# Hash attention and SwiGLU on one core: the second half of batch 1 takes its heads in turn with the first, and one more pair of heads is transposed by VectorE

## The chip, the core and the metric

The kernel runs on one core of one Trainium2 chip. The metric is the device time of one execution in microseconds (us). Before the change three runs gave 336.68, 337.49 and 340.18 us; their median is 337.49 us.

The core's engines run their own instruction streams in program order and meet at semaphores: TensorE (PE, matmuls and transposes), VectorE (DVE), ScalarE (ACT), GpSimd (POOL) and SyncE (SP, which in this kernel only issues DMAs). POOL issues the weights' DMAs.

## What is computed

The first half is attention with a hash mask, the second a gated feed-forward layer (FFN) over its rows. Cut to what matters:

```python
# q, k, v: (4 batches, 8 heads, 768 tokens, 64); proj: (64, 6)
q_bucket = sum over the 6 columns of (q @ proj > 0) * 2**column      # k_bucket likewise
scores = (q @ k.T) / 8
scores = where(q_bucket[:, None] == k_bucket[None, :], scores, -1e9)
attn = softmax(scores)                       # with 1e-9 added to the sum
attn_out = attn @ v
x = attn_out, heads side by side             # (3072, 512)
xn = x / sqrt(mean(x*x) + 1e-6) * rms_g
g = xn @ w_gate                              # 512 -> 1536
out = (g * sigmoid(g) * (xn @ w_val)) @ w_out
```

## The kernel before, in words

**Tiles.** The 768 queries of a batch are cut into two halves of 384, so there are eight windows `w` = 0 to 7, and window `w` belongs to batch `w // 2`. The eight heads of a batch are taken as four pairs `hp`; "(b,hp)" below is a pair of heads of batch b, "w2" is window 2. For each head of a window the 768 keys are taken in three parts.

**Attention.** One tile `QK` per pair holds, for each of its heads, 76 rows: 64 rows of q or k in fp16, transposed, and 12 rows of hash bits, so that one matmul gives score and mask together. `scores` (L338-347) is two matmuls of 384 columns, `probs` (L349) the exponential on ACT, `av` (L357) nine of the 18 matmuls with v, `attn_out` (L373) the division by the sum: VectorE writes `otmp` and `rcp`, POOL `x` and its square `sq` (for the last pair of w0 VectorE does all of it), and `sumsq` (L404) adds the squares up on VectorE.

**Preparing a pair** has two ways, told apart by the list `BY_PE` (L40).
- By PE: k and q come as rows, one DMA of 384 KB each (`load_rows`). `keep_pair` (L539) is called four times a pair, each time three fp32 transposes on PE and a copy out of PSUM by VectorE. `casts` (L543) writes fp16 into `QK`, by POOL, with a quarter of it on ACT. `hash_pair` (L585) makes the hash of both heads.
- By VectorE: k and q come in blocks of 32 columns, four DMAs of 96 KB each for k and for q (`load_blocks`, L115). `turn_dve` (L187) is called eight times a pair, four for k and four for q, each time one VectorE transpose of 128x192. `cast_pool` (L198) writes fp16 on POOL, two instructions for k and two for q. The hash of one pair is `hash_lone` (L273), that of two pairs `hash_pairs` (L288).
Either hash is matmuls `d_ps` on PE (L209), a comparison `bits` on VectorE (L216) and eight DMAs on SP that put the bits into `QK`, for one pair by `hash_pair` and `hash_lone` of 12x384, for two by `hash_pairs` of 12x768. The v of a pair is one DMA; `v_prep` (L307) casts it and `v_sum` (L311) adds it up, both on POOL; `v_mean` (L319) is a matmul of those sums and a VectorE copy `cvb`.

**FFN of a window.** `norm` (L410) makes the root mean square on VectorE and POOL, `scale_x` (L420, three times) `xn` on VectorE, `turn_x` (L425, three times) transposes it on PE and VectorE scales it into `xnT`. Then 12 steps `gate` (L436, four matmuls, tanh on ACT) and `value` (L450, four matmuls; VectorE makes `a` and then `ht`), and `project` (L464, nine calls of four matmuls; ACT copies the result out and SP stores it).

**The order** is written out by hand. `SLOTS` lists 192 slots, one per window, head and part of the keys; `plan[s]` holds what else is emitted in slot s, sorted by a rank. In slot s come `scores(s + 1)`, then the steps with rank under 3, then `probs(s + 1)`, then the others (L699-709). Every engine and each DMA queue runs its share in that order. The FFN of window w starts at slot 24w + 48: the first 16 slots from there hold gates and values, slots +16 to +24 the projection. So slots 48 to 63 carry gates and values of w0, 64 to 72 its projection, 72 to 87 those of w1, and so on.

`TURNS` (L33) gives the order of pairs in batch 0: w0 and w1 take turns. From w2 on a window's heads follow one another: w2 has slots 48 to 71, w3 72 to 95. Six pairs are in `BY_PE`: all of batch 0, (1,0) and (1,1).

**Buffers.** Loaded rows go through ten buffers (`lpool`, L61), each freed by its transposes or by `v_sum`. Banks of PSUM for everything but scores and `o_ps` are three (`gps`), so that a gate's matmuls wait until VectorE is done with a bank used three users before. `xpool` and `xnT` have two buffers, `xn` one. DMAs of SP share eight completion semaphores in turn, so that a DMA waits for the eighth one before it.

Of the kernel before, what the change touches and what calls it, by code (L numbers as in the profile page):

```python
# [15 lines left out]
H = 8  # L16
# [14 lines left out]


TURNS = [(0, 0), (1, 0), (0, 1), (1, 1), (0, 2), (0, 3), (1, 2), (1, 3)]  # L33
SLOTS = [(w, 2 * hp + hh, p) for w, hp in TURNS for hh in range(2) for p in range(3)]
SLOTS += [(w, h, p) for w in range(2, 8) for h in range(H) for p in range(3)]
NS = len(SLOTS)
LAST = {(w, h): g for g, (w, h, p) in enumerate(SLOTS) if p == 2}


BY_PE = [(0, hp) for hp in range(4)] + [(1, 0), (1, 1)]  # L40


@with_exitstack
def kernel(
# [12 lines left out]
    nc = tc.nc  # L57
# [40 lines left out]
    def raw_tile(b, hp, which):  # L98
        shape = [128, 24, 32] if which != "v" and (b, hp) not in BY_PE else [128, 2, 6, D]
        raw[b, hp, which] = lpool.tile(shape, FP32, name=which + "L", tag="L")  # L100
        return raw[b, hp, which]
# [39 lines left out]
    def k_cols(b, h, jt):  # L141
        o = (jt // 3) * S + (jt % 3) * 128 if (b, h // 2) in BY_PE else S + jt * 128
        return QK[b, h // 2][0:KROWS, h % 2, o : o + 128]

    def q_cols(w, h):
        b, half = divmod(w, 2)
        t = QK[b, h // 2][0:KROWS, h % 2]
        if (b, h // 2) in BY_PE:
            return t[:, half * S + HALF : (half + 1) * S]
# [4 lines left out]
    def v_chunk(b, h, jt):  # L154
        return 2 * (jt % 3) + jt // 3 if (b, h // 2) in BY_PE else jt

# [181 lines left out]
    def scores(g):  # L338
        w, h, p = SLOTS[g]
        ps = scps.tile([128, 2, 512], FP32, name="s_ps")  # L340
        idle(ps[:, 0, HALF:512], {0: 8, 3: 6}.get(g, 0))
        for j in range(2):
            nc.tensor.matmul(  # L343
                ps[:, j, 0:HALF], k_cols(w // 2, h, 2 * p + j), q_cols(w, h),
                start=True, stop=True,
            )
        sps[g] = ps

    def probs(g):  # L349
        w, h, p = SLOTS[g]  # L350
        if p == 0:
            psb[w, h] = ppool.tile([128, 3, 2, HALF], FP16, name="psb")
        nc.scalar.activation(  # L353
            psb[w, h][:, p], sps.pop(g)[:, :, 0:HALF], AF.Exp, scale=ESCALE,
        )
# [217 lines left out]
    def at(s, f, *a, rank=3):  # L573
        plan[s].append((rank, len(plan[s]), lambda: f(*a)))
# [39 lines left out]
        at(33 + 6 * i, load_wo, 6 * i, 6 * i + 6)  # L614

    for hp, loads, turns, sv in ((0, (9, 11, 15), (24, 26, 28, 30), 42),
                                 (1, (13, 17, 28), (33, 35, 37, 39), 45)):
        for which, s in zip("kqv", loads):  # L620
            at(s, load_rows, nc.sync, 1, hp, which)
        for i, s in enumerate(turns):
            at(s, keep_pair, 1, hp, i)
            at(s + 1, casts, 1, hp, i)
        at(turns[3] + 2, hash_pair, 1, hp)
        at(sv, v_prep, 1, hp)
        at(sv + 2, v_sum, 1, hp)

    def in_row(loads, s, hash_slot=None):
        return loads, range(s, s + 8), (s + 4, s + 8, s + 9), hash_slot

    work = {
        (1, 2): ((21, 23, 30), (36, 37, 40, 40, 48, 49, 50, 51), (42, 52, 46), 53),
        (1, 3): in_row((42, 44, 47), 52, 61),
        (2, 0): in_row((51, 56, 59), 61), (2, 1): in_row((64, 67, 70), 71, 80),
        (2, 2): in_row((73, 76, 79), 81), (2, 3): in_row((82, 85, 88), 91, 100),
        (3, 0): in_row((94, 98, 102), 106), (3, 1): in_row((104, 108, 112), 116, 125),
        (3, 2): in_row((116, 120, 124), 126), (3, 3): in_row((126, 130, 134), 136, 145),  # L640
    }
    for (b, hp), (loads, turns, cast_slots, sh) in work.items():
        for which, s in zip("kqv", loads):
            at(s, load_rows if which == "v" else load_blocks, nc.sync, b, hp, which)
        for i, s in enumerate(turns):
            at(s, turn_dve, b, hp, "kq"[i // 4], i % 4, rank=5)
        for which, s in zip("kq", cast_slots):
            at(s, cast_pool, b, hp, which)
        if sh:
            if b == 1:  # L650
                at(sh, hash_lone, b, hp)
            else:
                at(sh, hash_pairs, b, (hp - 1, hp))
        at(cast_slots[2], v_prep, b, hp)
        at(cast_slots[2], v_sum, b, hp)
        if hp % 2:
            at(66 if b == 1 else 48 * b + (17 if hp == 3 else -4), v_mean, b, hp - 1, 4)
    at(54, v_mean, 1, 0, 4)

    gts, sqs = {}, {}  # L660

# [13 lines left out]
    for w in range(8):  # L675
        for h in range(H):
            end = LAST[w, h] + 3
            at(end - 1, av, w, h, 0, 9)
            at(end, av, w, h, 9, 18)
            if h % 2:  # L680
                at(end, o_step, w, h // 2, rank=4.5)
                if (w, h) != (0, 7):
                    at(end + 6, s_step, w, h // 2, rank=5)
        at(end + (1 if w == 0 else 9), norm, w, rank=5)
        for c in range(3):
            at(end + (3 if w == 0 else 14 + c), scale_x, w, c, rank=5)
            at(end + (7 + c if w == 0 else 17 + 2 * c), turn_x, w, c, rank=1)
        s0 = 24 * w + 48
        seen = set()
        for ft in range(NF):  # L690
            for f, s in ((g_step, s0 + 16 * ft // NF), (v_step, s0 + (32 * ft + 16) // (2 * NF))):
                at(s, f, w, ft, rank=4 if s in seen else 2)
                seen.add(s)
        for i in range(9 if w < 7 else 6):
            c, j = divmod(i, 3)
            at(s0 + 16 + i, project, w, c, 4 * j, 4 * j + 4, rank=1 if i == 8 else 3)
# [61 lines left out]
```

## Time and profile before

| | before |
|---|---|
| runs | 336.68, 337.49, 340.18 us; median 337.49 |
| the profiled execution | 339.3 us, its span 337.5 us |
| granted TensorE clock | 0.999 |
| PE busy | 326.8 us (97%) |
| VectorE, ScalarE, POOL busy | 236.4 (70%), 210.0 (62%), 155.3 (46%) us |
| PE busy in 40 to 50, 50 to 60, 60 to 70 us | 8.98, 9.32, 7.84 of 10 us |
| PE busy in 70 to 80 and 80 to 90 us | 9.93, 10.00 of 10 us |
| chain that ended last | PE 85%, VectorE 6%, SP's queue 3%, DMA 2%, ACT 2% |

The span is the time from the first to the last instruction in the profile; the device time of that execution is 1.8 us longer. Times in rows of the timeline count from the span's start. A row gives the start, the busy time, the engine, the line, what is written and read, the count, and in brackets the idle time before it and what ended that. "PE" rows last until the result is out, so two of them overlap; the distance from start to start is what a matmul holds the engine for. "SPq" is SP's DMA queue.

### The profile page before, as it was taken

The numbers are of one execution on the slowest core, as the hardware profiler recorded it, in microseconds if no ns is written. First come the engines' busy times: TensorE is split into PE (matmuls) and PEld (weight loads), VectorE is DVE, ScalarE is ACT, GpSimd is POOL, SyncE is SP. The second block draws the span as 40 slices with busy tenths as digits, with TensorE's granted clock in tenths as the row PEclk, the third lists the DMA queues.
The fourth block names the chain that finished last, engine by engine and source line by source line (L and its number), as shares of the span: only waits on it lengthen the run. The fifth ranks groups of instructions, "written<-read, shape, count | busy, mean of one in ns | idle before, by whom it ended". The sixth has DMA issues, their size and how long they took to land.

```text
span 337.5 us, 7796 instructions
## 1 busy us (share of the span) xinstructions
PE 326.8 (97%) x2993; PEld 201.0 (60%) x2993; DVE 236.4 (70%) x526; ACT 210.0 (62%) x328; POOL 155.3 (46%) x230
## 2 busy tenths in 40 slices
PE   8999989889999999999999999999999999999995
PEld 7566656455566565566555666566556665655653
DVE  4769798688758896668768897557546663883860
ACT  3789987656666575757666676567667675332321
POOL 4878789836465576245736475613111311110000
PEclk9999999999999999999999999999999999999999
DMA  7999999464376064508243261100010001001002
GB/s 238 330 223 260 169 169 187 75 124 100 79 186 118 15 111 119 104 20 168 69 105 84 44 116 64 35 16 0 33 62 2 3 0 64 33 0 64 32 0 93
DMA packets 80244, 31.36 MB, mean 93 GB/s; under 512 B 65240, under 2 KB 77264, under 8 KB 80208
## 3 DMA queue, kind: packets, MB, share of 16 engines
q1 hardware_dynamic: 76272, 26.09, 31.7%
q0 software_dynamic: 3712, 4.72, 8.8%
q8 instruction: 23, 0.38, 0.5%
q14 instruction: 13, 0.11, 0.1%
q10 hardware_dynamic: 224, 0.07, 0.1%
HBM read 28.32 MB, written 6.29 MB: 103 GB/s over the span
## 4 chain that ended last, share of the span: by engine, by line
PE 85%; DVE 6%; SPq 3%; DMA 2%; ACT 2%; issue 1%; DVEq 0%; ACTq 0%
PE y_ps L469 18%; PE v_ps L455 17%; PE s_ps L343 15%; PE g_ps L445 12%; PE o_ps L365 9%; PE s_ps L445 5%; PE d_ps L209 4%; SPq L267 2%; PE t_ps L169 1%; PE x_ps L430 1%; PE z_ps L336 1%; DMA kL<-in_k_dram 1%; DVE otmp L380 1%; DVE xn L423 1%; ACT psb L353 1%
## 5 line engine op out<-in xcount | busy, mean ns | idle before, releaser
L353 ACT ACTIVATE psb<-s_ps 128x768 f16<-128x768 f32 x192 | 150.8, 808 | 28.1 <-PE s_ps L343 26.9
L343 PE MATMUL s_ps<-QK 76*128 76x384 f16 x384 | 93.5, 325 | 1.3 <-ACT psb L353 0.5
L455 PE MATMUL v_ps<-xnT,wv 128*128 128x384 f16 x384 | 78.1, 326 | 0.1
L469 PE MATMUL y_ps<-wo,ht 128*128 128x512 f16 x276 | 69.2, 379 | 0.3 <-ACT ysb L476 0.3
L389 POOL TENSOR_TENSOR x<-otmp,rcp 128x384 f32<-128x384 f32 x31 | 25.7, 830 | 93.0 <-DVE rcp L385 92.7
L365 PEld LDWEIGHTS <-psb 128*128 128x128 f16 x1152 | 51.6, 97 | 25.5 <-issue 7.5
L447 ACT ACTIVATE t<-g_ps 128x384 f32<-128x384 f32 x72 | 35.3, 490 | 43.6 <-PE g_ps L445 43.4
L458 DVE SCALAR_TENSOR_TENSOR ht<-a,v_ps 128x384 f16<-128x384 f32 x96 | 53.2, 554 | 10.7 <-PE v_ps L455 1.5
L457 DVE SCALAR_TENSOR_TENSOR a<-t,g_ps 128x384 f32<-128x384 f32 x72 | 39.5, 548 | 28.5 <-ACT t L447 28.3
L445 PE MATMUL g_ps<-xnT,wg 128*128 128x384 f16 x288 | 58.6, 325 | 0.7 <-DVE a L457 0.5
L365 PE MATMUL o_ps<-vl,psb 128*128 128x65 f16 x1152 | 56.8, 194 | 0.6 <-DVE otmp L380 0.5
L455 PEld LDWEIGHTS <-wv 128*128 128x128 f16 x384 | 36.4, 97 | 23.9 <-issue 0.5
L445 PEld LDWEIGHTS <-wg 128*128 128x128 f16 x384 | 36.0, 97 | 24.4 <-issue 1.1
L343 PEld LDWEIGHTS <-QK 76*128 76x128 f16 x384 | 31.6, 98 | 16.1 <-issue 3.7
L469 PEld LDWEIGHTS <-ht 128*128 128x128 f16 x276 | 25.9, 97 | 24.0 <-issue 0.6
L476 ACT COPY ysb<-y_ps 128x512 f32<-128x512 f32 x23 | 13.5, 585 | 25.5 <-PE y_ps L469 22.8
L431 DVE TENSOR_TENSOR xnT<-x_ps,gcol 128x512 f16<-128x512 f16 x24 | 16.3, 685 | 15.1 <-PE x_ps L430 15.1
L401 POOL TENSOR_TENSOR sq<-x 128x384 f32<-128x384 f32 x31 | 25.6, 826 | 2.4
L380 DVE TENSOR_TENSOR otmp<-o_ps,cvb 128x390 f32<-128x390 f32 x32 | 17.8, 558 | 8.8 <-PE o_ps L365 8.7
L447 ACT ACTIVATE t<-s_ps 128x384 f32<-128x384 f32 x24 | 11.8, 491 | 18.4 <-PE s_ps L445 17.6
L201 POOL CAST QK<-kT 64x768 f16<-64x768 f32 x20 | 16.8, 838 | 12.4 <-DVE kT L193 6.5
L193 DVE STREAM_TRANSPOSE kT<-kL 128x192 f32<-128x192 f32 x40 | 19.8, 517 | 2.7 <-DMA kL<-in_k_dram 2.7
(80 smaller groups left out, 325.7 us busy)
## 6 DMA issues: line engine op xcount, KB each, us to landing
vL<-in_v_dram SPq DMA_DIRECT2D x16, 384.0 KB
out_dram<-ysb SPq DMA_DIRECT2D x23, 256.0 KB
kL<-in_k_dram SPq DMA_DIRECT2D x40, 96.0 KB
qL<-in_q_dram SPq DMA_DIRECT2D x40, 96.0 KB
kL<-in_k_dram SPq DMA_DIRECT2D x5, 384.0 KB
qL<-in_q_dram SPq DMA_DIRECT2D x5, 384.0 KB
wg<-in_moe_w_gate_dram POOLq DMA_DIRECT2D x2, 768.0 KB, 7.2
wv<-in_moe_w_val_dram POOLq DMA_DIRECT2D x2, 768.0 KB, 8.5
```

The costliest lines, as they stand in the source:

```text
L343: nc.tensor.matmul(ps[:, j, 0:HALF], k_cols(w // 2, h, 2 * p + j), q_cols(w, h), start=True, stop=True,)
L353: nc.scalar.activation(psb[w, h][:, p], sps.pop(g)[:, :, 0:HALF], AF.Exp, scale=ESCALE,)
L365: nc.tensor.matmul(o[:, c, hh, 0:65], psb[w, h][:, jt // 2, jt % 2, 128 * c : 128 * c + 128], vls[b % 2][:, h, v_chunk(b, h, jt), 0:65], s ...
L380: nc.vector.tensor_add(tmp[:, :, :, 0:65], o[:, :, :, 0:65], cvb[b % 2][:, 2 * hp : 2 * hp + 2, 0:65].unsqueeze(1).to_broadcast([128, 3, 2 ...
L389: eng.tensor_mul(xd.rearrange("p c (h d) -> p c h d", h=2), tmp[:, :, :, 0:64], r.to_broadcast([128, 3, 2, 64]),)
L401: nc.gpsimd.tensor_mul(sq, xd, xd)
L445: nc.tensor.matmul(g, wg[:, kt, fs], xnT[w][:, kt], start=(kt == 0), stop=(kt == 3))
L447: nc.scalar.activation(t, g, AF.Tanh, scale=0.5)
L455: nc.tensor.matmul(vv, wv[:, kt, fs], xnT[w][:, kt], start=(kt == 0), stop=(kt == 3))
L457: nc.vector.scalar_tensor_tensor(out=a, in0=t, scalar=1.0, in1=g, op0=ALU.add, op1=ALU.mult)
L458: nc.vector.scalar_tensor_tensor(out=ht[w][:, ft], in0=a, scalar=0.5, in1=vv, op0=ALU.mult, op1=ALU.mult)
L469: nc.tensor.matmul(y, ht[w][:, ft, c * 128 : (c + 1) * 128], wo[:, ft, :], start=(ft == 0), stop=(ft == NF - 1),)
```

## The change

- `TURNS` is extended: w2 and w3 take turns by pairs exactly as w0 and w1. Batch 1 then goes (w2,pair 0), (w3,0), (w2,1), (w3,1), (w2,2), (w2,3), (w3,2), (w3,3), six slots each, from slot 48. The first use of pair (1,1) moves from slot 54 to 60, of (1,2) from 60 to 72, of (1,3) from 66 to 78.
- (1,1) leaves `BY_PE`: its k and q come in blocks, VectorE transposes them, POOL alone casts them, and its hash is `hash_lone` in slot 53 in place of `hash_pair` in slot 41. It takes the slots of turns and hash that (1,2) had. Its v is loaded in slot 33 (before 28), its q in slot 34 (before, as rows, in slot 17).
- Loads, turns and casts of (1,2), (1,3) and batch 2 move to later slots. The hash of (1,2) goes from slot 53 to 62, of (1,3) from 61 to 70, of (2,0) and (2,1) from 80 to 86, of (2,2) and (2,3) from 100 to 103.
- `v_mean` of batch 1 is four calls of two heads (slots 54, 62, 72, 80) in place of two of four heads (54 and 66).
- `norm` of w1 goes from slot 59 to 55 and its `scale_x` from 64-66 to 57-59; `norm` of w2 from 83 to 89 and its `scale_x` from 88-90 to 90-92. `turn_x` stays where it was in all windows. For w0, w1 and w2 the last `sumsq` comes three slots earlier after its pair.

The diff, without the lines that only rename:

```diff
 TURNS = [(0, 0), (1, 0), (0, 1), (1, 1), (0, 2), (0, 3), (1, 2), (1, 3)]
+TURNS += [(w + 2, hp) for w, hp in TURNS]
 SLOTS = [(w, 2 * hp + hh, p) for w, hp in TURNS for hh in range(2) for p in range(3)]
-SLOTS += [(w, h, p) for w in range(2, 8) for h in range(H) for p in range(3)]
+SLOTS += [(w, h, p) for w in range(4, 8) for h in range(H) for p in range(3)]
...
-BY_PE = [(0, hp) for hp in range(4)] + [(1, 0), (1, 1)]
+BY_PE = [(0, hp) for hp in range(4)] + [(1, 0)]
...
-    for hp, loads, turns, sv in ((0, (9, 11, 15), (24, 26, 28, 30), 42),
-                                 (1, (13, 17, 28), (33, 35, 37, 39), 45)):
-        for which, s in zip("kqv", loads):
-            at(s, load_rows, nc.sync, 1, hp, which)
-        for i, s in enumerate(turns):
-            at(s, keep_pair, 1, hp, i)
-            at(s + 1, casts, 1, hp, i)
-        at(turns[3] + 2, hash_pair, 1, hp)
-        at(sv, v_prep, 1, hp)
-        at(sv + 2, v_sum, 1, hp)
+    for which, sl in zip("kqv", (9, 11, 15)):
+        at(sl, load_rows, nc.sync, 1, 0, which)
+    for i, sl in enumerate((24, 26, 28, 30)):
+        at(sl, keep_pair, 1, 0, i)
+        at(sl + 1, casts, 1, 0, i)
+    at(32, hash_pair, 1, 0)
+    at(42, v_prep, 1, 0)
+    at(48, v_sum, 1, 0)
...
     work = {
-        (1, 2): ((21, 23, 30), (36, 37, 40, 40, 48, 49, 50, 51), (42, 52, 46), 53),
-        (1, 3): in_row((42, 44, 47), 52, 61),
-        (2, 0): in_row((51, 56, 59), 61), (2, 1): in_row((64, 67, 70), 71, 80),
-        (2, 2): in_row((73, 76, 79), 81), (2, 3): in_row((82, 85, 88), 91, 100),
-        (3, 0): in_row((94, 98, 102), 106), (3, 1): in_row((104, 108, 112), 116, 125),
+        (1, 1): ((21, 34, 33), (36, 37, 40, 40, 48, 49, 50, 51), (46, 52, 55), 53),
+        (1, 2): in_row((42, 45, 47), 53, 62), (1, 3): in_row((50, 53, 56), 61, 70),
+        (2, 0): in_row((58, 62, 64), 69), (2, 1): in_row((67, 70, 73), 77, 86),
+        (2, 2): in_row((76, 79, 82), 86), (2, 3): in_row((84, 87, 90), 94, 103),
+        (3, 0): in_row((95, 98, 102), 106), (3, 1): in_row((104, 108, 112), 116, 125),
         (3, 2): in_row((116, 120, 124), 126), (3, 3): in_row((126, 130, 134), 136, 145),
     }
...
-        if hp % 2:
-            at(66 if b == 1 else 48 * b + (17 if hp == 3 else -4), v_mean, b, hp - 1, 4)
-    at(54, v_mean, 1, 0, 4)
+        if b > 1 and hp % 2:
+            at(48 * b + (17 if hp == 3 else -4), v_mean, b, hp - 1, 4)
+    for hp, s in enumerate((54, 62, 72, 80)):
+        at(s, v_mean, 1, hp, 2)
...
                 if (w, h) != (0, 7):
-                    at(end + 6, s_step, w, h // 2, rank=5)
-        at(end + (1 if w == 0 else 9), norm, w, rank=5)
+                    at(end + (3 if h == 7 and w < 3 else 6), s_step, w, h // 2, rank=5)
+        s0 = 24 * w + 48
+        n0 = {0: 9, 1: 17, 2: 7}.get(w, 13)
+        at(s0 - n0, norm, w, rank=5)
         for c in range(3):
-            at(end + (3 if w == 0 else 14 + c), scale_x, w, c, rank=5)
-            at(end + (7 + c if w == 0 else 17 + 2 * c), turn_x, w, c, rank=1)
-        s0 = 24 * w + 48
+            at(s0 - {0: 7, 1: 15 - c, 2: 6 - c}.get(w, 8 - c), scale_x, w, c, rank=5)
+            at(s0 - (3 - c if w == 0 else 5 - 2 * c), turn_x, w, c, rank=1)
```

In a row of `work` the numbers are the slots of the loads of k, q and v, of the eight turns (`in_row` takes eight slots in a row from its second number), of the casts of k, q and v (4, 8 and 9 slots after the first turn by `in_row`), and of the hash.

## The prediction

> **What bounds the kernel now.** I read the page's busy shares first, then the busy times of chosen stretches, then the timelines of PE, VectorE, POOL and SP around the slots that the diff names, then the DMA queues there.
>
> ```profile
> PE 326.8 (97%) x2993; PEld 201.0 (60%) x2993; DVE 236.4 (70%) x526; ACT 210.0 (62%) x328; POOL 155.3 (46%) x230
> ...
> 41.00:55.40 14.40, 12.89 (x165) 8.71 (x162) 13.66 (x33) 11.76 (x18) 11.58 (x18) 1.00 1.05 189
> 60.00:70.00 10.00, 7.84 (x65) 4.23 (x64) 6.92 (x17) 4.84 (x9) 6.49 (x10) 1.00 0.63 111
> 69.10:84.00 14.90, 14.83 (x137) 8.99 (x137) 12.78 (x29) 9.53 (x16) 8.04 (x11) 1.00 0.54 110
> 98.40:121.90 23.50, 23.50 (x226) 14.56 (x224) 20.36 (x46) 16.23 (x28) 12.38 (x18) 1.00 0.40 78
> ```
>
> In the rows of stretches the columns are length, then PE, PEld, VectorE, ACT and POOL. PE bounds the kernel: 97% of the span, and all of it once the FFN runs (23.50 of 23.50 us in slots 73 to 87). Two stretches that the change touches are different: slots 33 to 47 (41.0 to 55.4), where VectorE is the busiest engine with 13.66 of 14.40, and 60 to 70, where PE is busy for only 7.84. The second holds a standstill:
>
> ```profile
> 64.44 0.51 PE L209 MATMUL d_ps<-kT,pk 128*32 128x384 f32 x1
> ...
> 65.23 0.45 PE L365 MATMUL o_ps<-vl,psb 128*128 128x65 f16 x9
> ...
> 65.84 0.81 PE L455 MATMUL v_ps<-xnT,wv 128*128 128x384 f16 x4
> 68.30 0.29 PE L324 MATMUL m_ps<-vsum,ones 128*128 128x260 f16 x1 [1.65 <-DVE bits L216]
> 69.10 0.81 PE L445 MATMUL g_ps<-xnT,wg 128*128 128x384 f16 x4 [0.51 <-DVE a L457]
> ...
> 67.28 0.52 DVE L193 STREAM_TRANSPOSE kT<-kL 128x192 f32<-128x192 f32 x1 [2.73 <-DMA kL<-in_k_dram]
> 67.64 0.60 DVE L216 TENSOR_SCALAR bits<-d_ps,thr,scl 128x384 f16<-128x384 f32 x1
> ...
> 34.62 6.73 SPq L121 DMA_DIRECT2D kL<-in_k_dram  x4
> ...
> 46.65 14.63 SPq L267 DMA_DIRECT2D QK<-bits  x16
> 61.39 3.06 SPq L121 DMA_DIRECT2D kL<-in_k_dram  x4
> ...
> 78.40 0.65 PE v_ps L455 x4
> ```
>
> Read from the end: SP spends 46.65 to 61.28 on the 16 DMAs of two `hash_pair`s, so the k load of (1,3), emitted in slot 42, is issued only at 61.39. In slot 52 VectorE takes its first transpose of that load and waits 2.73 us; the hash of slot 53 (`bits`) and the FFN's `a` stand behind it in VectorE's queue. PE waits for their PSUM banks. Four matmuls of 384 columns hold PE 0.65 us by the chain that ended last (the row at 78.40), so PE was free at 66.49, began `m_ps` at 68.30 and the next gate at 69.10: 1.8 + 0.7 = 2.5 us lost.
>
> **The change, part by part.**
>
> *The standstill goes: -2.5 us.* The second `hash_pair`'s eight DMAs leave slot 41, and the transposes behind `hash_lone` in slot 53 are now those of k of (1,2), again emitted in slot 42. Of the queue ahead, eight DMAs remain (slot 32). They can start when their `bits` are there, since SP is done with the k blocks of slot 21 at 41.35 (the row at 34.62); 8 x 14.63/16 = 7.3 us bring SP to about 49, one v and four q issues (3.06/4 = 0.77 each) to 53, and k of (1,2) is issued by 56 to 58. It is wanted at about 63. So I count the whole 2.5 as won; bounds 0 and -2.5.
>
> *Slots 33 to 47: PE, ACT and VectorE lose work, worth at most 1.6 us.* Twelve fp32 transposes of `keep_pair` leave PE, six small casts leave POOL and two ACT, and four copies out of PSUM leave VectorE. PE and ACT are not the limit here, so what counts is the chain to the first gate of w0 at 56.03:
>
> ```profile
> 44.86 0.56 DVE L177 COPY kT<-t_ps 128x384 f32<-128x384 f32 x1
> ...
> 48.77 0.54 DVE L177 COPY qT<-t_ps 128x384 f32<-128x384 f32 x1
> 49.23 0.15 DVE L412 TENSOR_REDUCE ss<-ssp 128x3 f32<-128x12 f32 x1
> ...
> 50.83 2.67 DVE L423 TENSOR_SCALAR xn<-x,rstd 128x512 f16<-128x512 f32 x3
> ...
> 54.11 1.87 DVE L431 TENSOR_TENSOR xnT<-x_ps,gcol 128x512 f16<-128x512 f16 x3
> ...
> 56.03 0.81 PE L445 MATMUL g_ps<-xnT,wg 128*128 128x384 f16 x4 [0.18 <-DVE xnT L431]
> ...
> L423 DVE TENSOR_SCALAR xn<-x,rstd x24: 399/482/1046, 50.8 to 304.0; 128x512 f16<-128x512 f32 x24
> ```
>
> The two copies shown stand in that chain; from 48.77 to `ss` at 49.23 one is worth 0.46, so 0.9 for both. The three `xn` take 2.67, while the median of all 24 is 0.48 each; if POOL's missing casts let them run nearer the median, another 0.7 is possible. Gain at the first gate: 0.9 to 1.6. But it meets the next item.
>
> *The q load of (1,1): a new wait, which eats nearly all of that.* It is emitted in slot 34, behind the eight hash DMAs and the v of (1,1); VectorE wants it in slot 48:
>
> ```profile
> 58.53 0.92 DVE L193 STREAM_TRANSPOSE qT<-qL 128x192 f32<-128x192 f32 x2
> ...
> 61.86 0.54 DVE L457 SCALAR_TENSOR_TENSOR a<-t,g_ps 128x384 f32<-128x384 f32 x1
> ...
> 62.72 0.81 PE L455 MATMUL v_ps<-xnT,wv 128*128 128x384 f16 x4
> ...
> 44.09 0.89 POOL L526 DMA_DIRECT2D wo<-in_moe_w_out_dram  x1
> 44.97 1.06 POOL L185 CAST QK<-kT 64x384 f16<-64x384 f32 x2
> 45.98 0.51 POOL L185 CAST QK<-qT 64x384 f16<-64x384 f32 x1
> 46.52 1.28 POOL L185 CAST QK<-kT 64x384 f16<-64x384 f32 x2
> 47.75 0.82 POOL L526 DMA_DIRECT2D wo<-in_moe_w_out_dram  x1
> ```
>
> The casts between the two loads of `wo` are (1,1)'s and go, so both `wo` loads (768 KB each) are issued by about 46. What a weight load on POOL's queue q0 does to blocks on SP's queue q1 is seen in 36 to 40, with the second `wv` load, then in 40 to 44 without it, and with `wo` in 47.5 to 57.5:
>
> ```profile
> q0 software_dynamic: 440, 0.68, 102.3%
> q1 hardware_dynamic: 63, 0.01, 2.6%
> ...
> q1 hardware_dynamic: 4074, 0.51, 85.6%
> ...
> q0 software_dynamic: 1543, 1.55, 96.5%
> q1 hardware_dynamic: 524, 0.52, 18.8%
> ```
>
> The columns are packets, MB and share. Block loads issued at 34.62 moved 63 packets until 40, then 4074 in the next 4 us: they wait until the weights are through. An estimate for q of (1,1): q0 moves 0.68/4 = 0.17 MB per us, or about 0.2 when alone in full flow, from some 2.7 us after its issue; 1.57 MB from 46.8 end at about 55; v (0.39 MB) takes 1 us more and the q blocks (0.39 MB at 0.51 per 4 us, somewhat faster in full flow) 2 to 3, so q lands between 57.8 and 59.5; I take 58.6. VectorE would want it at 57.6 (58.53 less 0.9). From the first q transpose to the end of the third `a` VectorE works 62.40 - 58.53 = 3.9 us without a break, and the value matmuls at 62.72 need the bank which that `a` frees. So PE is there at landing + 3.9, or 62.5: 0.2 better than before. Both items together -0.2; bounds -1.6 (q lands before 57) and +2.2 (lands at 61, if SP or `wo` are late).
>
> The Trainium skill, "DMA: Bandwidth & Descriptors", section "Queues, rings and completion order", says that each DMA engine serves its queues in turn, a packet at a time. By that rule the q blocks would share with `wo` instead of following it; the rows at 36 to 40, 63 packets against 440, show no even turn.
>
> *One more hash where PE is the limit: +0.8.* The hash of (1,1) went in slot 41, beside VectorE's chain. Now three `hash_lone` (slots 53, 62, 70) lie after slot 48 where two did. One holds PE from 64.44 to 65.23, 0.8 us. Nothing covers it there.
>
> *VectorE in slots 48 to 63: +0.3.* Eight transposes replace four copies, but slots 48 to 63 have 15 transposes before and after. New there are the three `scale_x` of w1 (slots 57 to 59, before 64 to 66), 3 x 0.48 = 1.4 us and more where they run slow. In slots 73 to 87 VectorE is busy 20.36 of 23.50 with 13 transposes, so some 3 us are idle, though in pieces. I take 0.3, between 0 and 1.1 (all of it, if VectorE is still behind from slot 48).
>
> *At nothing:* the halved `v_mean` (same columns, two instructions more); POOL's cast of (1,1) (four casts for six smaller); the order of heads itself, since each window's FFN keeps its slot and its norm comes before it. Two places have little left. `norm` of w2 is in slot 89, two slots before PE wants `xn`; if POOL is late PE stands there. The hash of (2,2) and (2,3) is four slots ahead of its use instead of seven:
>
> ```profile
> 109.75 1.43 PE d_ps L209 x16
> ...
> 111.95 6.86 SPq L302 DMA_DIRECT2D QK<-bits  x8
> ...
> 72.83 1.79 DMA QK<-bits
> ```
>
> From the matmuls to the first issue 2.2 us, the first two issues 2 x 0.86, landing 1.8 less an issue: 5 us, against about 6.5 us (3.5 slots of some 1.5 us and the hash's own 1.4). Cover 1.5 us.
>
> **Sum.** -2.5 - 0.2 + 0.8 + 0.3 = -1.6 us against the span of 337.5. The profiled execution took 339.3, 1.8 more than its span; the median of the runs, 337.49, happens to equal the span, so I set the sum against it: 335.9 us.
>
> **The rivals.**
>
> *The wait moves (the other side).* Place: VectorE's first q transpose of (1,1) in slot 48. Price: each us that the load lands after 58.6 costs PE one. From 60.2 on the sum is not below before; at 62 the time is 339.3. For it: SP's k blocks of slot 21 took 6.73 us to issue while weights were moving, and the q blocks now meet two weight loads back to back. Against it: everything ahead of it on SP is done by 49, and after `wo` blocks come at 1 MB in 8 us.
>
> *The load comes in time.* Blocks get a turn beside `wo`, q lands before 57, the first gate comes 1.2 us earlier and no lag is left for slots 57 to 63: -2.5 - 1.2 + 0.8 = -2.9, 334.6; with the full 1.6 and nothing lost, 334.2. For it: in 47.5 to 57.5 q1 did move 0.52 MB beside `wo`. Against it: the 63 packets. The rule of the Trainium skill named above would give this too.
>
> *VectorE takes over the bound in slots 57 to 63,* as it has `scale_x`, a transpose in each slot and the FFN's pairs: +1.1 for 0.3, 336.7. For it: VectorE's 12.78 of 14.90 us at 69.10 to 84, before the three `xn` come in. Against it: PE lost only 0.07 us there.
>
> **How the numbers follow.** Forecast 0.5, wait moves 0.15, load in time 0.2, VectorE bounds 0.15. The likeliest gives 335.9. Bounds: 334.2 less what the fastest of the three runs lay under the median (0.8) gives 333.4; above, 337.5 - 2.5 + 2.2 + 0.8 + 1.1 = 339.1. About 1% (3.4 us) is what a measurement of this kernel can tell from no change. Under 334.1 comes only part of "in time" and little else: 0.15. Over 340.9 needs the load at 63.6 or a hidden stall in slot 91 or 107: 0.08. The rest, 0.77.
>
> **What would show it.** Right: no `DMA kL` ahead of a VectorE transpose in 60 to 70, and PE busy over 9.5 of 10 there; the first gate near 55; a wait for `DMA qL` of 1 us or so at the first q transpose; three hashes of 0.8 us between 60 and 95. Wrong: that wait at 3 us or more, gaps in PE at slots 57 to 63 behind `a` or `ht`, PE idle before `x_ps` of w2 or before the scores of slot 107 behind `bits`; or a first gate as late as before, which would mean that something else than VectorE's chain sets it.

## The result and the profile after

| | before | after |
|---|---|---|
| median of the runs, us | 337.3 (336.68 to 340.18, 6 runs) | 341.75 (341.3 to 342.43, 6 runs) |
| ratio after to before | | 1.0113, 95% interval 1.0067 to 1.0158 |
| profiled execution and its span, us | 339.3, 337.5 | 341.3, 339.5 |
| PE busy | 326.8 us (97%) | 325.7 us (96%) |

The change made the kernel 1.1% slower. The prediction said 335.9, at most 339.1. Of the 77 timed executions of before in all sessions, 44 took 336.4 to 337.9 us and the others 338 to 344; the profile that the prediction read (339.3) is one of the longer ones. So the kernel before was profiled twice more in the experiments; below, "the usual execution" is the first of these (336.98, span 335.2).

Two of the stretches shown before, in after (columns as there):

```profile
41.00:55.40 14.40, 12.44 (x156) 8.20 (x153) 10.67 (x29) 12.12 (x18) 8.59 (x12) 1.00 0.93 152
60.00:70.00 10.00, 7.42 (x62) 4.15 (x62) 8.71 (x21) 3.72 (x7) 5.99 (x8) 1.00 0.86 149
```

The second of them in the usual execution of before:

```profile
60.00:70.00 10.00, 9.82 (x94) 5.79 (x92) 9.04 (x20) 5.96 (x11) 6.40 (x11) 1.00 0.86 153
```

In the first stretch VectorE falls from 13.66 to 10.67 of 14.40 us. The second holds the surprise. PE is busy for 7.42 of 10 in after, much as in the profile that the prediction read (7.84), but for 9.82 in the usual execution: the standstill that the change was to remove is not there in the usual execution, and after has one of its own. The timeline of after on PE, VectorE, SP and POOL:

```profile
53.80 0.81 PE L446 MATMUL g_ps<-xnT,wg 128*128 128x384 f16 x4 [0.41 <-DVE xnT L432]
...
58.25 0.49 PE L344 MATMUL s_ps<-QK 76*128 76x384 f16 x2
61.47 0.81 PE L456 MATMUL v_ps<-xnT,wv 128*128 128x384 f16 x4 [2.73 <-DVE a L458]
...
64.02 0.81 PE L456 MATMUL v_ps<-xnT,wv 128*128 128x384 f16 x4 [0.49 <-DVE a L458]
...
47.98 0.17 DVE L413 TENSOR_REDUCE ss<-ssp 128x3 f32<-128x12 f32 x1
...
49.45 1.83 DVE L424 TENSOR_SCALAR xn<-x,rstd 128x512 f16<-128x512 f32 x3 [0.53 <-POOL rstd L419]
...
55.83 0.55 DVE L459 SCALAR_TENSOR_TENSOR ht<-a,v_ps 128x384 f16<-128x384 f32 x1
60.17 0.85 DVE L194 STREAM_TRANSPOSE qT<-qL 128x192 f32<-128x192 f32 x2 [3.79 <-DMA qL<-in_q_dram]
...
41.59 6.58 SPq L268 DMA_DIRECT2D QK<-bits  x8
...
48.83 8.08 SPq L122 DMA_DIRECT2D qL<-in_q_dram  x4
57.00 3.54 SPq L122 DMA_DIRECT2D kL<-in_k_dram  x4
...
44.08 1.71 POOL L527 DMA_DIRECT2D wo<-in_moe_w_out_dram  x2
```

VectorE is free for the first q transpose of (1,1) at 56.38 (55.83 + 0.55) and gets it at 60.17, after 3.79 us. The FFN's `a` stands behind it, and PE, which waits for that, does nothing from 58.7 to 61.47 (the wait of 2.73 before `v_ps`). The same instructions of PE in the usual execution of before, the first gate and the fourth value, and further on the gate of slot 54, the value of slot 72 and the first `x_ps` of w2:

```profile
55.89 0.81 PE L445 MATMUL g_ps<-xnT,wg 128*128 128x384 f16 x4 [0.41 <-DVE xnT L431]
...
62.57 0.81 PE L455 MATMUL v_ps<-xnT,wv 128*128 128x384 f16 x4
...
66.80 0.81 PE L445 MATMUL g_ps<-xnT,wg 128*128 128x384 f16 x4 [0.18 <-DVE a L457]
...
95.47 0.81 PE L455 MATMUL v_ps<-xnT,wv 128*128 128x384 f16 x4
...
124.11 0.39 PE L430 MATMUL x_ps<-ident,xn 128*128 128x128 f16 x4
```

and the last three in after, with what stands around them:

```profile
68.62 0.81 PE L446 MATMUL g_ps<-xnT,wg 128*128 128x384 f16 x4 [0.61 <-DVE a L458]
...
92.75 0.51 PE L210 MATMUL d_ps<-kT,pk 128*32 128x384 f32 x1
...
93.53 1.04 PE L470 MATMUL y_ps<-wo,ht 128*128 128x512 f16 x4
...
98.84 0.81 PE L456 MATMUL v_ps<-xnT,wv 128*128 128x384 f16 x4 [0.38 <-DVE cvb L328]
...
128.76 0.40 PE L431 MATMUL x_ps<-ident,xn 128*128 128x128 f16 x4 [0.95 <-DVE xn L424]
...
67.62 0.49 DVE L406 TENSOR_REDUCE ssp<-sq 128x3 f32<-128x384 f32 x1
...
98.49 0.29 DVE L328 TENSOR_SCALAR cvb<-m_ps 128x130 f32<-128x130 f32 x1 [1.91 <-PE m_ps L325]
...
127.68 1.02 DVE L424 TENSOR_SCALAR xn<-x,rstd 128x512 f16<-128x512 f32 x1 [0.73 <-POOL rstd L419]
```

Subtracting start from start tells where the time went. At the first gate after is ahead by 2.1 us (55.89 - 53.80). At the fourth value it is behind by 1.45 (64.02 - 62.57): the q wait cost 3.5. At the value of slot 72 it is behind by 3.4 (98.84 - 95.47): the third lone hash in slot 70 (92.75 to 93.53), the `v_mean` of (1,2), after which PE stands for 0.4 us, and 0.4 in slot 54. There the gate waits 0.61 us for VectorE's `a` instead of 0.18: the last `sumsq` of w1 (67.62), which the change puts three slots earlier, stands ahead of it. At `x_ps` of w2 it is behind by 4.65: PE waits 0.95 us for the first `xn`. About 0.5 of that is caught up in slot 94, and the span ends 4.3 us behind (339.5 - 335.2).

### The profile page after: what moved, and what is told of

Its sections match the earlier page's. It is cut to its first block, busy times and chain, and to the rows that moved or that the text cites. A ratio compares the mean times of both kernels' runs of the same rounds, so it can differ in the third digit from the quotient of the medians.

```text
span 339.5 us, 7782 instructions
## 1 busy us (share of the span) xinstructions
PE 325.7 (96%) x2983; PEld 199.4 (59%) x2983; DVE 237.1 (70%) x532; ACT 209.1 (62%) x326; POOL 155.3 (46%) x228
## 4 chain that ended last, share of the span: by engine, by line
PE 83%; DVE 7%; DMA 4%; ACT 3%; SPq 1%; issue 1%; POOL 0%; DVEq 0%; POOLq 0%; ACTq 0%
PE v_ps L456 17%; PE y_ps L470 17%; PE s_ps L344 15%; PE g_ps L446 12%; PE o_ps L366 9%; PE s_ps L446 5%; PE d_ps L210 4%; ACT psb L354 2%; DMA qL<-in_q_dram 2%; PE x_ps L431 1%; SPq L122 1%; PE t_ps L170 1%; DMA vL<-in_v_dram 1%; DVE otmp L381 1%; PE z_ps L337 1%
## 5 line engine op out<-in xcount | busy, mean ns | idle before, releaser
L202 POOL CAST QK<-qT 64x768 f16<-64x768 f32 x22 | 18.2, 827 | 16.5 <-DVE qT L194 15.9
L194 DVE STREAM_TRANSPOSE qT<-qL 128x192 f32<-128x192 f32 x44 | 21.5, 512 | 3.8 <-DMA qL<-in_q_dram 3.8
```

Of the source, the lines that this page charges most:

```text
L194: nc.vector.transpose(dst.rearrange("p (c t r) -> p r c t", c=6, r=4)[:, r : r + 1], src.rearrange("p (r c) d -> p r c d", r=4)[:, r : r + 1],
```

## The experiments

Theory A: a usual execution of before has no standstill in slot 54, so there was nothing to win there, and after pays for a q load that waits behind the weights. Rivals: the standstill is real and after loses elsewhere; the q load waits for SP's own queue and not for the weights; the order of the heads costs nothing.

**1 and 2. The kernel before, unchanged, profiled again twice.** No edit.

> The kernel before, unchanged, for another profile of it. Its runs lie at 336.7 to 337.5 and at 339.3 to 340.2 us, and the profile that the prediction read is one of the slower ones (339.3, span 337.5). Theory A: the standstill of PE at 66.5 to 69.1 is in every execution; then a profile with a device time near 337 shows it too, and the 2 us lie elsewhere. Theory B: the standstill is what tells the two apart; then a profile near 337 has a span of about 335.5 and VectorE does not wait 2.7 us for the k load of (1,3), and a profile near 339.5 does.

> The kernel before, unchanged, once more, so that both kinds of execution may be seen. The same two theories as for the first: by A both profiles have the wait for the k load in slot 52 whatever their time, by B it is there (2 to 3 us) only if the device time is near 339.5.

Measured 336.98 and 337.07, spans 335.2 and 335.3. SP's queue and VectorE in the first of them:

```profile
44.88 13.09 SPq L267 DMA_DIRECT2D QK<-bits  x16
58.08 3.21 SPq L121 DMA_DIRECT2D kL<-in_k_dram  x4
...
63.85 0.56 DVE L458 SCALAR_TENSOR_TENSOR ht<-a,v_ps 128x384 f16<-128x384 f32 x1
64.32 0.58 DVE L193 STREAM_TRANSPOSE kT<-kL 128x192 f32<-128x192 f32 x1
```

The k load of (1,3) is issued at 58.08 instead of 61.39, as the 16 hash DMAs begin 1.8 us sooner and take 13.09 instead of 14.63, and VectorE's first transpose of it follows `ht` without a wait. The other profile shows the same (issue at 57.44). Between the profile that the prediction read and these two, the starts of PE's score matmuls differ by 2.2 us in slot 54 and by nearly nothing elsewhere. So the standstill is real, but neither of the two usual executions has it. It is shown for one longer execution; whether all longer ones have it, no run shows.

**3. The q load of (1,1) early.** The changed kernel with one slot moved:

```diff
-        (1, 1): ((21, 34, 33), (36, 37, 40, 40, 48, 49, 50, 51), (46, 52, 55), 53),
+        (1, 1): ((21, 23, 33), (36, 37, 40, 40, 48, 49, 50, 51), (46, 52, 55), 53),
```

> The changed kernel with one number altered: the q blocks of (1,1) are emitted in slot 23 instead of 34, right behind its k blocks and ahead of the eight hash DMAs of (1,0). Theory A (q waits behind the weights): the blocks move at 42 to 47 us, before the first wo load starts, the 3.8 us wait of VectorE at 56.4 goes and with it PE's 2.9 + 0.65 us in slots 51 to 53: span 339.5 - 3.5 = 336.0, device time 337.8. Theory B (VectorE is the limit from slot 48 on whatever comes first): the loss comes back behind a later instruction of slots 50 to 63 and the span stays at 338.5 or more.

Measured 337.66 (10 runs), ratio to before 1.0003 (0.9982 to 1.0023), span 335.9. SP and VectorE:

```profile
41.49 2.67 SPq L122 DMA_DIRECT2D qL<-in_q_dram  x4
...
56.32 0.89 DVE L194 STREAM_TRANSPOSE qT<-qL 128x192 f32<-128x192 f32 x2
```

The q blocks are issued ahead of the `wo` loads, in 2.67 us, and the transposes begin at 56.32 without a wait. The span falls by 3.6 us: the wait accounts for most of what after lost.

**4. The second `wo` load late, the q load where the change put it.**

```diff
-        at(33 + 6 * i, load_wo, 6 * i, 6 * i + 6)
+        at((33, 56)[i], load_wo, 6 * i, 6 * i + 6)
```

> The changed kernel with the second wo load issued in slot 56 instead of 39; the q load of (1,1) stays in slot 34. Theory A (it is the second weight load that holds the q blocks up): the first wo load ends near 51, v and q blocks move from 51 to 55, VectorE waits 0 to 0.5 us in place of 3.8, span 336.0 to 336.6. Theory B (SP's queue holds them up: eight hash DMAs and v go first, and the issues themselves are slow): q still lands near 59 and the span stays within 0.5 of 339.5.

Measured 338.53 (10 runs), ratio 1.0016 (0.9992 to 1.004), span 336.7. SP still holds the q load behind eight hash DMAs and the v load:

```profile
41.48 6.17 SPq L268 DMA_DIRECT2D QK<-bits  x8
...
48.33 4.08 SPq L122 DMA_DIRECT2D qL<-in_q_dram  x4
...
56.18 0.91 DVE L194 STREAM_TRANSPOSE qT<-qL 128x192 f32<-128x192 f32 x2
```

The issues begin within 0.5 us of those in after, take 4.08 instead of 8.08, and VectorE does not wait. SP's queue ahead of the load is therefore not the cause; the second weight load is. Nor is it the eight completion semaphores that hold SP in after: the DMAs whose semaphores the third and fourth block reuse had landed by 47.2 and 50.7, and their issues end at 53.9 and 56.9. (With the second `wo` load late, PE loses 0.7 us in slot 73 instead, behind a copy on ACT, which is why this kernel is behind experiment 3.)

**5. The order alone.** The changed kernel, but (1,1) is transposed by PE as before; the new order of heads and the moved steps stay.

```diff
-BY_PE = [(0, hp) for hp in range(4)] + [(1, 0)]
+BY_PE = [(0, hp) for hp in range(4)] + [(1, 0), (1, 1)]
...
+                                     (1, (13, 17, 28), (33, 35, 37, 39), 45, 47)):
...
-        (1, 1): ((21, 34, 33), (36, 37, 40, 40, 48, 49, 50, 51), (46, 52, 55), 53),
```

> The changed kernel with the new order of heads, the new slots of norm, scale_x, turn_x and v_mean and the later loads, but with pair (1,1) turned by PE as in the kernel before (loads in 13, 17, 28, keep_pair in 33 to 39, hash_pair in 41, v_prep in 45, v_sum in 47). There are then two lone hashes after slot 48, as before, no q wait of (1,1), and no gain at the first gate. Theory A (the order and the moved steps cost by themselves: 0.6 in slot 72, 1.1 less 0.5 in slot 91): span 335.2 + 1.2 = 336.4, device 338.2, 0.8 to 1.4 above the kernel before. Theory B (the order is at nothing, as the prediction had it, and VectorE's turning of (1,1) carries all of the loss): device 337.0 to 337.4, as before.

Measured 337.81 (10 runs), ratio 1.0008 (0.9986 to 1.0031); the profiled execution 338.12, span 336.3. PE in slots 72 (the value) and 91:

```profile
95.85 0.81 PE L456 MATMUL v_ps<-xnT,wv 128*128 128x384 f16 x4 [0.38 <-DVE cvb L328]
...
125.76 0.40 PE L431 MATMUL x_ps<-ident,xn 128*128 128x128 f16 x4 [0.96 <-DVE xn L424]
```

Both waits are there without any VectorE transposes of (1,1), so they belong to the order and the moved steps, and the first gate comes at 56.06, much as in the usual execution (55.89). The span is 1.1 above the usual execution's, but 0.6 of that is there before the edits can matter: the first scores start at 8.85 instead of 8.22. What is left, 0.5, is less than theory A's 0.8 to 1.4; it is the sum of the two waits, less what is caught up and some smaller gains. The medians, 0.4 apart with an interval from -0.5 to +1.0, don't exclude theory B's total by themselves.

**6. The v work of (2,1) earlier on POOL**, with the early q load.

```diff
-(2, 1): in_row((67, 70, 73), 77, 86),
+(2, 1): ((67, 70, 73), range(77, 85), (81, 85, 83), 86),
```

> The changed kernel with q of (1,1) loaded in slot 23 and, new, v_prep and v_sum of (2,1) in slot 83 instead of 86. In the changed kernel, and in the one with the early q load alone (span 335.9), PE loses 1.1 us in slot 91, where it waits for the first xn of w2; POOL works on v_prep and v_sum of (2,1) from 121.0 to 123.9 and only then squares the sums of w2 (sq at 124.7, rstd at 126.8). Theory A: POOL's order makes rstd late; with 2.8 us of v work moved ahead, the wait goes and PE gains 0.6 (1.1 less the 0.5 that is caught up in slot 94 anyhow) to 1.1: span 334.8 to 335.3, device 336.6 to 337.1, no wait of PE for xn of w2 over 0.2 us. Theory B: rstd is late because the slot of the norm is late, or the first xn is slow beside POOL's cast (1.02 us instead of 0.40): the wait stays at 0.7 to 1.1 and device stays at 337.6.

Measured 337.73 (12 runs), ratio 0.9997 (0.9976 to 1.0019), span 335.7. VectorE, POOL and PE:

```profile
120.86 1.22 DVE L194 STREAM_TRANSPOSE kT<-kL 128x192 f32<-128x192 f32 x3
121.92 0.49 DVE L406 TENSOR_REDUCE ssp<-sq 128x3 f32<-128x384 f32 x1
...
120.03 0.83 POOL L402 TENSOR_TENSOR sq<-x 128x384 f32<-128x384 f32 x1
122.71 0.20 POOL L415 TENSOR_SCALAR ms<-ss 128x3 f32<-128x3 f32 x1 [1.85 <-DVE ss L413]
...
124.96 0.40 PE L431 MATMUL x_ps<-ident,xn 128*128 128x128 f16 x4 [0.94 <-DVE xn L424]
```

My theory fell: `sq` is ready 1.1 us before VectorE adds it up, POOL now idles for 1.85 us, and PE waits as long as before. VectorE's own order, three transposes ahead of the sum of squares, held it.

**7. `v_mean` of (1,2) two slots later**, on top of 6.

```diff
-    for hp, s in enumerate((54, 62, 72, 80)):
+    for hp, s in enumerate((54, 62, 74, 80)):
```

> The kernel before in this list and, on top, v_mean of (1,2) in slot 74 instead of 72. In the changed kernel PE waits in slot 72 behind that v_mean (0.6 us against the kernel before), because VectorE frees its bank late. Theory A: two slots later VectorE has air and the 0.6 go: device 0.4 to 0.6 under the kernel before in this list, 336.1 to 336.6, and below the kernel before the change (337.2 to 337.6) by about 0.3 %. Theory B: the wait belongs to VectorE's queue as a whole in slots 70 to 76 and only moves to slot 74: no difference over 0.2.

Measured 337.13 (12 runs), ratio 0.9988 (0.9961 to 1.0016). PE no longer stands at the value of slot 72. The medians, 0.6 apart, don't show it beyond the noise; the starts of the score matmuls do: 0.6 us is won there and 0.5 of it kept to the end, as theory A had it. Its reason was wrong: the row of `cvb` in after shows that VectorE had been idle for 1.91 us and copied at once. In slot 72 the value's matmuls stand right behind `m_ps` and wait for that copy, by their row; that they need its bank is inferred. In slot 74 nothing behind `m_ps` waits.

**8 and 9. The norm of w2**, on top of 7: `norm_early` moves the last sum of squares and the norm one slot up, `norm_turns` also takes (2,2)'s transposes and casts out of the way.

```diff
-at(end + (3 if h == 7 and w < 3 else 6), s_step, ...)
+at(end + (2 if h == 7 and w == 2 else 3 if h == 7 and w < 3 else 6), s_step, ...)
-        n0 = {0: 9, 1: 17, 2: 7}.get(w, 13)
+        n0 = {0: 9, 1: 17, 2: 8}.get(w, 13)
# norm_turns only
-(2, 2): in_row((76, 79, 82), 86),
+(2, 2): ((76, 79, 82), (86, 89, 90, 91, 92, 93, 94, 95), (94, 97, 97), None),
```

> The kernel with v_mean of (1,2) in slot 74 and, of the steps of the run beside it, only the earlier sum of squares and norm of w2 (slot 88), which puts them ahead of one transpose of (2,2); the cast of (2,2) on POOL still follows rstd at once, so the first xn still runs beside it. Theory A (VectorE's order and the cast each hold a part): PE's wait of 0.94 us falls by one transpose, 0.35 to 0.4, and the first xn still takes about 1.0 us; device 336.8 to 337.1. Theory B (the cast alone): the wait stays over 0.8.

> The changed kernel with the early q load of (1,1), v_prep and v_sum of (2,1) in 83, v_mean of (1,2) in 74 (device 337.1 so far), and now the last sum of squares and the norm of w2 one slot earlier (88), the transposes of (2,2) in 86, 89 to 95 instead of 86 to 93, its casts in 94, 97, 97. So far VectorE takes three transposes of (2,2) (1.22 us) between its last ht and the sum of squares, though sq was ready at 121.05; then ss, POOL's ms and rstd, and a first xn that takes 1.02 us beside POOL's cast of (2,2) where another takes 0.41; PE waits 0.94 us. Theory A: these two things are the whole wait: the sum of squares comes 1 us earlier, xn runs at 0.4, PE waits under 0.2 us before x_ps of w2, and device falls by 0.4 (if half is caught up later anyhow, as the 0.5 in slot 94) to 1.0: 336.1 to 336.7. Theory B: PE is so close to its limit after slot 91 that the wait is only moved (to m_ps, to the scores behind late casts): no difference over 0.2.

Measured 336.75 and 336.22 (12 runs each); ratios in that session 0.9927 (0.9893 to 0.996) and 0.994 (0.9916 to 0.9963), against a kernel before whose executions there were mostly of the longer kind (median 339.09); the two intervals overlap, so they don't order the two kernels. Against the medians of before in the other sessions, 337.3 to 337.6, the better one is 0.3 to 0.4% faster, which is no comparison within one session, and its span of 334.4 lies 0.8 below the usual execution's 335.2. `norm_early`, then `norm_turns`:

```profile
122.79 1.02 DVE L424 TENSOR_SCALAR xn<-x,rstd 128x512 f16<-128x512 f32 x1 [0.49 <-POOL rstd L419]
...
122.71 1.79 POOL L202 CAST QK<-kT 64x768 f16<-64x768 f32 x2
...
123.88 0.40 PE L431 MATMUL x_ps<-ident,xn 128*128 128x128 f16 x4 [0.60 <-DVE xn L424]
```

```profile
122.61 0.49 DVE L424 TENSOR_SCALAR xn<-x,rstd 128x512 f16<-128x512 f32 x1 [0.47 <-POOL rstd L419]
...
123.56 0.39 PE L431 MATMUL x_ps<-ident,xn 128*128 128x128 f16 x4
```

Theory A holds for both, though the first median lies 0.05 us under its range: one transpose less takes PE's wait from 0.94 to 0.60, and without the cast beside it the first `xn` takes 0.49 instead of 1.02 and the wait is gone.

**10. The kernel before with the k load of (1,3) two slots earlier**, to see whether that makes the longer executions go.

```diff
-        (1, 3): in_row((42, 44, 47), 52, 61),
+        (1, 3): in_row((40, 44, 47), 52, 61),
```

> The kernel before with the k load of (1,3) in slot 40 instead of 42, so that its four issues stand on SP's queue ahead of the eight hash DMAs of (1,1) in slot 41. In the profile that the prediction read, those issues came at 61.39 and VectorE waited 2.73 us for them; in two other profiles of the same kernel they came at 58.08 and 57.44 and nobody waited. Theory A: that wait is what makes the longer executions of the kernel before (338 to 340, about one in four): with the load ahead of the hash DMAs they go or get rarer, the usual time stays where it is (336.5 to 337.8), and the profile has no wait for k of (1,3). Theory B: the longer executions have another cause: they stay as frequent. Theory C (the prediction's): the standstill is there in every execution: the usual time falls by 2.5 to about 335.

Measured 342.03 (338.83 to 344.43, 6 runs), ratio 1.0113 (1.0071 to 1.0156): none of the three, since no run took less than 338.83. SP and PE of the profiled execution (338.83):

```profile
52.03 5.98 SPq L121 DMA_DIRECT2D kL<-in_k_dram  x4
58.10 6.61 SPq L267 DMA_DIRECT2D QK<-bits  x8
...
75.25 0.48 PE L343 MATMUL s_ps<-QK 76*128 76x384 f16 x2 [1.34 <-DMA QK<-bits]
```

The k blocks, now issued beside the `wo` loads, hold SP for 5.98 us, the hash DMAs of (1,1) behind them start at 58.10, and the scores at 75.25 wait for them, 1.34 us on PE. The five other runs had a granted clock of 0.988 to 0.995 where the profiled one had 0.999; why, no run tells. What makes some executions of before longer is not settled by this.

## Why the prediction was wrong, step by step

- **"The standstill goes: -2.5 us": the step that failed.** The mechanism was read rightly from its profile, and the cure works: k of (1,2) is issued at 57.00 in after and nobody waits for it. But the stall is in neither usual execution of before that was profiled (experiments 1 and 2), while the time to be predicted is a median of these. The sign was there to see: the profiled execution took 339.3, 1.8 above the median and as much above its own span. The prediction noticed that the median "happens to equal the span", set the sum against it, and so took a stall out of a median that did not hold one. The usual execution has a span of 335.2 and ends at 336.98, again span + 1.8. Against 337.3 this step was worth about 0. The prediction gave the step bounds of 0 and -2.5, but its upper end, 339.1, takes the full -2.5; with 0 it would have been 341.6.
- **Slots 33 to 47, gain 0.9 to 1.6:** right in kind, larger: 2.1, or 2.2 against the profile that the prediction read. By its rows `ss` comes 1.25 earlier (49.23 to 47.98; the copies were put at 0.9) and the three `xn` take 0.84 less (2.67 to 1.83; put at up to 0.7).
- **The q load, both items together -0.2:** the wait was in the right place, and its rule, PE at the landing + 3.9, holds (60.17 + 3.9 = 64.07, measured 64.02). The sizes were off: VectorE wanted the blocks at 56.38 instead of 57.6, as the gate came earlier, and could start at 60.17 instead of 58.6, so the wait was 3.8 instead of 1.0. A part of that is the issue: the sum let SP issue the four q blocks in 3.06 us, they took 8.08, and the last was out at 56.91 instead of 53. The two items gave +1.45; that is within the bounds, -1.6 and +2.2. Experiment 4 shows the mechanism, the second weight load. This is the rival "the wait moves", whose arithmetic (not below before from 60.2 on) rested on the 2.5.
- **One more hash, +0.8:** right: PE's hash in slot 70 takes 0.78.
- **VectorE, +0.3:** the number is right by luck. The 0.4 is lost in slot 54, behind the `sumsq` of w1 that the change moved there and the prediction did not price; the `scale_x` of w1 in slots 57 to 59, its reason, cost nothing: from slot 55 to 61 after stays 1.8 us behind the usual execution.
- **At nothing:** the hash of (2,2) and (2,3) indeed cost nothing. `v_mean` cost 0.6, by its slot and not by its size (experiments 5 and 7). The norm of w2 was named as a place with "little left" and yet put at nothing; it cost 1.1, about 0.5 of it caught up. POOL's v work, moved away in experiment 6, was not the reason; VectorE's order and the slow `xn` beside POOL's cast were (experiments 8 and 9). The order of heads, put at nothing too, cost 0.5 us in all, moved steps included (experiment 5).

Put right with these values, 0 + 1.45 + 0.8 + 0.4 + 0.6 + 0.6 = +3.9 on the usual 336.98 gives 340.8; the profiled execution of after took 341.3, so 0.5 us is left unexplained.

## What to carry to other kernels

Before a stall is counted as a gain, see whether the profiled execution is a usual one: its own device time (its span plus what lies around it, here 1.8 us in every run) must meet the median. A span that meets the median, as here, is a sign of the opposite. If the device time does not meet it, look for the stall in a second profile. A load that VectorE or PE needs soon is better issued ahead of large weight loads on another queue than behind them: here that was worth 3.6 us of span. A step put "at nothing" with little slack deserves a price: two of these came to 1.2 us here.

## What the hardware showed

**Blocks on one queue wait for weight loads on another.** The DMA queues of after in 47 to 50, 50 to 53, 53 to 56 and 56 to 60 (packets, MB, share); q0 carries `wo`, q1 the hash rows, v, q and at the end k:

```profile
q0 software_dynamic: 507, 0.52, 114.2%
q1 hardware_dynamic: 10, 0.01, 0.9%
...
q0 software_dynamic: 530, 0.53, 106.7%
q1 hardware_dynamic: 140, 0.11, 15.0%
...
q0 software_dynamic: 407, 0.42, 81.4%
q1 hardware_dynamic: 402, 0.33, 43.5%
...
q1 hardware_dynamic: 3774, 0.47, 80.2%
q0 software_dynamic: 61, 0.05, 7.0%
```

Ten packets against 507, then 140 against 530, then 402 against 407, and 3774 once `wo` is through. The Trainium skill, "DMA: Bandwidth & Descriptors", section "Queues, rings and completion order", lets each DMA engine serve its queues in turn, a packet at a time; the rows of 53 to 56 agree with that, those of the first 6 us show no even turn. How much q1 had ready there (v was issued at 48.27) was not counted. An even turn in packets is none in bytes for the blocks: from 56 on q1's packets are 0.125 KB on average (0.47 MB in 3774), those of `wo` 1 KB (0.42 MB in 407). The issue stalls as well: four q blocks hold SP for 8.08 us beside two weight loads, 4.08 with the second one late, 2.67 ahead of them, and whatever stands behind on SP waits with it.

**A scaling on VectorE takes twice as long beside a cast on POOL:** the first `xn` of w2 1.02 us beside it, 0.49 without. The Trainium skill, "SBUF — State Buffer", section "Who interferes with whom", describes a port pair that VectorE, in its 2-port modes, and GpSimd can't hold at once: whoever issues first has it for the whole instruction, and the other waits. The rows agree with that, as the cast began first (122.71 against 122.79); whether `xn` ran in such a mode, no row tells.
